# Sums of g's blocks for the seven-product matrix multiply: from VectorE to accumulating transfers on GpSimd's queue, with signs chosen anew

## The chip, the cores and the metric

The kernel runs on one core of one Trainium2 chip. The metric is device microseconds of one execution. A core has five engines that run in parallel, each taking its own instructions in program order: TensorE (PE in the profile; its weight loads are PEld), VectorE (DVE), ScalarE (ACT), GpSimd (POOL) and SyncE (SP). Transfers are issued from an engine's queue and carried out by 16 DMA engines. Engines wait for each other, and for transfers, by semaphores.

## The reference

Two blocks follow one another. The first is a linear attention (RWKV6): per head and time step, `y[t] = r[t] @ (state + (u*k[t]) outer v[t])` and `state = w[t] * state + k[t] outer v[t]`, with 4 batches, 8 heads, 768 steps and 48 channels. Its output, taken as `x` of 3072 tokens by 384, goes through a two-layer network:

```python
h = x @ w_in                                   # w_in: 384 x 2048
g = 0.5 * h * (1.0 + erf(h * inv_sqrt2))       # exact GELU
out = (g @ w_out).astype(np.float32)           # w_out: 2048 x 384
```

Everything is float32. The change lies in how `g @ w_out` is computed.

## The kernel before

**Chunks.** The 3072 tokens are worked in eight chunks of T = 384 tokens, numbered 0 to 7. `attention(x + 1)` is generated in step with `mlp(x)`: both are Python generators, and a string of letters per chunk (`PLAN`) says which one issues its next piece. A letter "." takes a step of `mlp`, "f" and "s" take steps of the attention, "l" a load, "w" and "x" sums of the weights and of x. So the order of every engine's instructions is written out by hand; no scheduler moves them. Chunk 7's `mlp` has no attention left beside it and ends the kernel.

**g.** In `mlp(x)` the activations lie transposed: 2048 rows of g as 16 blocks of 128 partitions, by tokens. Four tiles `gs[0]` to `gs[3]` hold four such blocks each (`[128, 4, 384]`). In even chunks the last 128 tokens are kept in a tile `alone` instead, which waits there for the odd chunk behind it. So an odd chunk has 128 + 128 tokens and then a second pair: its own last 128 and the 128 of `alone`.

**Seven products.** For a pair of 128-token blocks, `g @ w_out` is a 2 x 2 by 2 x 2 block product, done in seven products instead of eight (Winograd's form of Strassen's scheme). With a00, a01 for the first token block (its two halves of the 2048) and a10, a11 for the second, the sums on g's side are

    s1 = a10 + a11,   s2 = s1 - a00,   s3 = a00 - a10,   and later  s2 <- a01 - s2

and on the side of the weights three sums `t` in `sums`, made once (`w_sums`, L873, and `first_sum`, L882). One product is eight matmuls of 128x192, one for each block row of 128 (`product`, L1235, its matmul is L1237); the profile shows two records for a float32 matmul, so a product is "x16". The order within a pair, all on the in-order TensorE, is: p1 (a00), o2 (a11), o1 (a01), **fourth: s2**, fifth: s1, sixth: s3, **seventh: the later s2**. In an odd chunk the second pair follows with five more: a11, s2, s1, s3, later s2. Each sum has two halves, k = 0 and 1, one tile of 128 x 512 float32 (256 KB) each; a product reads half 0 in its first four matmuls and half 1 in its last four.

**Where the sums are made.** `of_g(k)` (L997) makes s1, s2 and s3 of half k with three VectorE instructions (L1003, L1005, L1007). In chunks 2 to 6 half 0 is called for after the last but one group of h, and half 1 right after p1, since the last GELUs (`rest`, called between the halves of p1) come only then. In chunk 1 both are called in the h loop (L1231). In chunk 7 `of_g(0)` is the entry "sums" of `ORDER15` and `of_g(1)` follows the last own product. The later s2 is L1291, after the fifth product has been issued. An odd chunk's second pair gets its sums at L1302 and L1303 (after the sixth product), L1311 (after the seventh) and L1350. s1 lies in the tiles named f, s2 in those named e, s3 in the one named s; tile names in the profile are of the buffer's first user.

Of the kernel before, what the change touches and what calls it, by code (L numbers as in the profile page):

```python
# [17 lines left out]
AF = mybir.ActivationFunctionType  # L18
ALU = mybir.AluOpType
# [45 lines left out]
def kernel(  # L65
# [25 lines left out]
    nc = tc.nc  # L91
# [41 lines left out]
    def bank(name="o_ps"):  # L133
        return ps.tile([128, BANK], F32, name=name, tag="mm", bufs=2)
# [13 lines left out]
    alone = bufs[0][:, ALL:ALL + NF * 128].rearrange("p (f t) -> p f t", f=NF)  # L148
# [132 lines left out]
    for i, h in enumerate(QUARTERS[:1]):  # L281
        for a in range(3):
            w_q = (3 - a) * C // 4
            z = q_ints[1 if a == 0 else 2]
            o = i * C if a < 2 else i * C + C // 2
# [580 lines left out]
    HF, HM = NF // 2, DM // 2  # L866
    FG = 4
    sums, s3_sb = [], []

    def w_quarter(b, c, k):  # L870
        return w_out_sb[:, b * HF + k * FG:b * HF + (k + 1) * FG, c * HM:(c + 1) * HM]

    def w_sums():  # L873

        sums.extend(cv.tile([128, HF, HM], F32, name="t", tag="raw", bufs=AHEAD) for _ in range(3))
        for out_, x, y in ((0, (0, 1), (0, 0)), (1, (1, 1), (0, 1)), (0, (1, 1), 0), (2, (1, 0), 0)):
            for k in range(2):
                o = sums[out_][:, k * FG:(k + 1) * FG]
                nc.vector.tensor_sub(o, w_quarter(*x, k), sums[y][:, k * FG:(k + 1) * FG] if isinstance(y, int) else w_quarter(*y, k))
                yield  # L880

    def first_sum():  # L882
        for k in range(2):
            nc.vector.tensor_sub(w_quarter(0, 1, k), w_quarter(0, 1, k), w_quarter(0, 0, k))
            yield


# [2 lines left out]
    s_of, x_sums, s12_of, s_both = [], [], {}, []  # L890
# [91 lines left out]
    def mlp(x):  # L982
# [5 lines left out]
        waits, ends = x % 2 == 0, x % 2 == 1  # L988
        gs = {}
# [4 lines left out]
        def store(row0, o_sb, c0=0):  # L994
            nc.sync.dma_start(out=out[row0:row0 + 128, c0:c0 + o_sb.shape[1]], in_=o_sb)

        def of_g(k):  # L997

            s1.append(s12_of["s1"][k])
            s2.append(s12_of["s2"][k])  # L1000
            s3.append(s3_sb[0][:, k * FG:(k + 1) * FG])
            a00, a10, a11 = (gs[g][:, :, a:a + 128] for g, a in ((k, 0), (k, 128), (k + 2, 128)))
            nc.vector.tensor_add(s1[k], a10, a11)  # L1003
            yield
            nc.vector.tensor_sub(s2[k], s1[k], a00)  # L1005
            yield
            nc.vector.tensor_sub(s3[k], a00, a10)  # L1007
            yield

        def multiply(o, lhsT, rhs, start=False):  # L1010
# [4 lines left out]
        def h_halves():  # L1015
# [101 lines left out]
            for _ in of_g(0):  # L1117
                pass
# [93 lines left out]
        s1, s2, s3 = [], [], []  # L1212
# [22 lines left out]
        def product(o, lhs, rhs, start=False):  # L1235
            for j in range(HF):
                nc.tensor.matmul(o, lhsT=lhs(j), rhs=rhs(j), start=start and j == 0, stop=(j == HF - 1),  # L1237
                                 skip_group_check=True)
                if j == HF // 2 - 1:
                    yield  # L1240

        def of_sums(s):
            return lambda j: s[j // FG][:, j % FG, :]

        def of_t(i):
            return lambda j: sums[i - 1][:, j, :]

        def of_blocks(a, b):
            return lambda j: block(a, b, j)
# [4 lines left out]
        def of_w(b, c):  # L1254
            return lambda j: w_out_sb[:, b * HF + j, c * HM:(c + 1) * HM]

        def psum():
            return bank()[:, 0:HM]

        def two_rows():  # L1260
            return [wk.tile([128, DM], F32, name="o_sb", bufs=2) for _ in range(2)]
# [3 lines left out]
        if halves:  # L1265
            o_sb = two_rows()
            p1, u2, u3 = (wk.tile([128, HM], F32, name=name, bufs=1) for name in ("p1", "u2", "u3"))
            o1, o2 = psum(), psum()
            for _ in product(o1, of_blocks(0, 0), of_w(0, 0), True):
                yield  # L1270
                for z in late:
                    z()
            nc.scalar.copy(out=p1, in_=o1)
            if late:
                for _ in of_g(1):
                    pass
            yield
            yield from product(o2, of_blocks(1, 1), of_t(3), True)
            nc.scalar.copy(out=o_sb[1][:, 0:HM], in_=o2)
            yield  # L1280
            yield from product(o1, of_blocks(0, 1), of_w(1, 0))
            nc.scalar.copy(out=o_sb[0][:, 0:HM], in_=o1)
            yield
            yield from product(o2, of_sums(s2), of_t(1), True)
            nc.vector.tensor_add(u2, o2, p1)
            yield
            yield from product(o1, of_sums(s1), of_w(0, 1), True)
            nc.scalar.copy(out=o_sb[1][:, HM:], in_=o1)
            for k in range(2):

                nc.vector.tensor_sub(s2[k], gs[k + 2][:, :, 0:128], s2[k])  # L1291
            yield
            yield from product(o2, of_sums(s3), of_t(2))
            nc.vector.tensor_add(u3, o2, p1)
            for c in range(2):
                z = o_sb[1][:, c * HM:(c + 1) * HM]
                nc.vector.tensor_add(z, z, u3)
            store(row0 + 128, o_sb[1])
            if ends:
                s1 = s12_of["s1"]  # L1300
                for k in range(2):
                    nc.vector.tensor_add(s1[k], gs[k][:, :, 256:], gs[k + 2][:, :, 256:])  # L1302
                    nc.vector.tensor_sub(s3[k], alone[:, k * FG:(k + 1) * FG], gs[k][:, :, 256:])  # L1303
            yield
            yield from product(o1, of_sums(s2), of_w(1, 1))
            nc.vector.tensor_add(o_sb[0][:, HM:], o1, u2)
            store(row0, o_sb[0])
            if ends:
                s2 = s12_of["s2"]
                for k in range(2):  # L1310
                    nc.vector.tensor_sub(s2[k], s1[k], alone[:, k * FG:(k + 1) * FG])  # L1311
            yield
        else:
            o_ps = [bank()[:, 0:DM] for _ in range(2)]
            for f in range(NF):
                for i, o in enumerate(o_ps):
                    nc.tensor.matmul(o, lhsT=block(i, f // HF, f % HF), rhs=w_out_sb[:, f, :],
                                     start=(f == 0), stop=(f == NF - 1))
                if f < NF - 1:
                    yield  # L1320
            for i, o in enumerate(o_ps):
                o_sb = wk.tile([128, DM], F32, name="o_sb", bufs=2)
                nc.scalar.copy(out=o_sb, in_=o)
                store(row0 + i * 128, o_sb)
            yield

        if waits:
            _, o2, o1 = psum(), psum(), psum()
            o_sb = wk.tile([128, DM], F32, name="o_sb", bufs=2)
            yield from product(o2, of_alone(0), of_w(0, 0), True)  # L1330
            nc.scalar.copy(out=p1_alone, in_=o2)
            yield
            yield from product(o1, of_alone(1), of_w(1, 0), True)
            nc.vector.tensor_add(o_sb[:, 0:HM], o1, p1_alone)  # L1334
            store(row0 + 256, o_sb[:, 0:HM])
            yield
        elif ends:
            o_sb = two_rows()
            p1, u2, u3 = p1_alone, *(wk.tile([128, HM], F32, name=name, bufs=1) for name in ("u2", "u3"))
            o2, o1 = psum(), psum()  # L1340
            yield from product(o1, of_blocks(2, 1), of_t(3), True)
            nc.scalar.copy(out=o_sb[1][:, 0:HM], in_=o1)
            yield
            yield from product(o2, of_sums(s2), of_t(1), True)
            nc.vector.tensor_add(u2, o2, p1)
            yield
            yield from product(o1, of_sums(s1), of_w(0, 1), True)
            nc.scalar.copy(out=o_sb[1][:, HM:], in_=o1)
            for k in range(2):
                nc.vector.tensor_sub(s2[k], alone[:, HF + k * FG:HF + (k + 1) * FG], s2[k])  # L1350
            yield
            yield from product(o2, of_sums(s3), of_t(2))
            nc.vector.tensor_add(u3, o2, p1)
            for c in range(2):
                z = o_sb[1][:, c * HM:(c + 1) * HM]
                nc.vector.tensor_add(z, z, u3)  # L1356
            store(row0 + 256, o_sb[1])
            yield
            yield from product(o1, of_sums(s2), of_w(1, 1))
            nc.vector.tensor_add(o_sb[0][:, 0:HM], o1, u2)  # L1360
            store(row0 - T + 256, o_sb[0][:, 0:HM], HM)
            yield
# [114 lines left out]
```

## Time and profile before

| | |
|---|---|
| runs | 589.09, 589.76, 591.12 us; median 589.76 |
| profiled execution | 591.24 us, span of the instructions 589.5 us |
| granted TensorE clock, mean | 0.997 |
| busy: PE / PEld / DVE / ACT / POOL | 571.5 / 508.5 / 462.6 / 275.7 / 8.0 us |
| transfers | 46.80 MB, mean 79 GB/s |
| VectorE's sums of g | L1003 9.6, L1005 9.7, L1007 9.6 (x14 each), L1291 9.0 (x14), L1302 5.5, L1303 5.5, L1311 5.1, L1350 5.1 (x8 each) us |

Busy time is the time in which an engine had an instruction in work. A line "A <- B" of the waits says for what the engine A stood idle, in total, how often, and the longest once. The chain of work that ended last is followed back from the last instruction. Times in timelines are microseconds from the span's start.

### The profile page before, as it was taken

To read this page: it belongs to the slowest core of one execution; us is meant where nothing else is said; L and a number is where in the kernel's file an instruction comes from. 1 tells how busy PE (TensorE), PEld (TensorE's weight loads), DVE (VectorE), ACT (ScalarE), POOL (GpSimd) and SP (SyncE) were. 2 spreads that over 40 slices of the span, in tenths; PEclk is the share of its full clock that TensorE was granted. 3 is DMA by queue.
4 is the path that set the end of the run, shared out by engine and by line. 5 is a ranking of instruction groups with operands and counts; after the bars stand their busy time and mean duration, and the time that the engine had idled before them with its cause. 6 is when DMAs were issued, how large, how long until landed. Compare 5 with 4: busy or idle time off the path is not lost. (4 is left out here: it accounts for less than half of the span.)

```text
span 589.5 us, 17409 instructions
## 1 busy us (share of the span) xinstructions
PE 571.5 (97%) x7497; PEld 508.5 (86%) x7509; DVE 462.6 (78%) x907; ACT 275.7 (47%) x640; POOL 8.0 (1%) x21
## 2 busy tenths in 40 slices
PE   5789999999999999999999999999999999999998
PEld 3566666766799999999999999999999999999997
DVE  5879767988969987787859987688768998985532
ACT  2267889323612458045461468235461465523400
POOL 3100000000000000000000000000000000000000
PEclk9999999999999999999999999999999999999999
DMA  6649571020152201341023410421015200210000
GB/s 238 193 156 342 193 267 56 31 91 1 23 147 78 77 34 28 101 126 38 0 40 104 126 37 16 100 79 43 2 26 170 73 2 2 41 39 8 1 14 34
DMA packets 51004, 46.80 MB, mean 79 GB/s; under 512 B 31728, under 2 KB 36080, under 8 KB 50928
## 3 DMA queue, kind: packets, MB, share of 16 engines
q1 hardware_dynamic: 50832, 45.62, 25.5%
q8 instruction: 59, 0.97, 0.7%
q14 instruction: 17, 0.14, 0.1%
q10 hardware_dynamic: 96, 0.07, 0.1%
HBM read 36.24 MB, written 4.72 MB: 69 GB/s over the span
## 5 line engine op out<-in xcount | busy, mean ns | idle before, releaser
L1011 PE MATMUL h_ps<-xT,w_in_sb 128*128 128x192 f32 x408 | 81.2, 330 | 0.5 <-DVE o_sb L1334 0.3
L1011 PEld LDWEIGHTS h_ps<-xT,w_in_sb 128*128 128x128 f32 x408 | 67.8, 190 | 3.5 <-ACT g L1043 1.2
L1223 PE MATMUL h_ps<-xT,w_in_sb 128*128 128x384 f32 x192 | 64.4, 490 | 0.4 <-DMA xT<-ysb 0.4
L1223 PEld LDWEIGHTS h_ps<-xT,w_in_sb 128*128 128x128 f32 x192 | 35.8, 190 | 24.6 <-DMA xT<-ysb 1.0
L1237 PE MATMUL o_ps<-w_out_sb,g 128*128 128x192 f32 x224 | 39.5, 326 | 0.0
L1237 PEld LDWEIGHTS o_ps<-w_out_sb,g 128*128 128x128 f32 x224 | 37.0, 190 | 0.3
L620 ACT COPY a_sb<-d 32x256 f32<-32x256 f32 (+8 forms) x90 | 32.6, 362 | 4.6 <-PE d L604 3.1
L465 PEld LDWEIGHTS d<-rkw 64*64 64x64 f32 x1152 | 20.8, 147 | 16.0 <-issue 11.2
L1237 PE MATMUL o_ps<-w_out_sb,f 128*128 128x192 f32 x176 | 31.7, 330 | 0.0
L465 PE MATMUL d<-rkw 64*64 64x64 f32 (+1 forms) x1152 | 23.5, 234 | 8.2 <-DMA rkw<-in_rkw_dram 3.9
L1237 PE MATMUL o_ps<-t,g 128*128 128x192 f32 x176 | 31.4, 329 | 0.0
L1237 PE MATMUL o_ps<-w_out_sb,e 128*128 128x192 f32 x176 | 31.3, 328 | 0.0
L1237 PE MATMUL o_ps<-t,s 128*128 128x192 f32 x176 | 30.9, 327 | 0.0
L1237 PE MATMUL o_ps<-t,e 128*128 128x192 f32 x176 | 30.9, 327 | 0.0
L637 DVE COPY_PREDICATED a_sb<-quarter,d 128x480 f32<-128x480 uint8 (+5 forms) x54 | 23.2, 439 | 8.6 <-PE d L604 7.3
L764 DVE SCALAR_TENSOR_TENSOR st<-st,tot_sb,kv_ps 128x48 f32<-128x48 f32 x160 | 28.9, 259 | 0.9 <-PE kv_ps L749 0.8
L1011 PE MATMUL u_ps<-s,w_in_sb 128*128 128x192 f32 x160 | 29.5, 327 | 0.0
L1237 PEld LDWEIGHTS o_ps<-t,g 128*128 128x128 f32 x176 | 28.7, 190 | 0.4
L1237 PEld LDWEIGHTS o_ps<-w_out_sb,f 128*128 128x128 f32 x176 | 28.7, 190 | 0.4
L1237 PEld LDWEIGHTS o_ps<-w_out_sb,e 128*128 128x128 f32 x176 | 28.8, 190 | 0.3
L1237 PEld LDWEIGHTS o_ps<-t,s 128*128 128x128 f32 x176 | 28.8, 190 | 0.1
L1237 PEld LDWEIGHTS o_ps<-t,e 128*128 128x128 f32 x176 | 28.8, 190 | 0.1
(236 smaller groups left out, 1166.8 us busy)
## 6 DMA issues: line engine op xcount, KB each, us to landing
rkw<-in_rkw_dram SPq DMA_DIRECT2D x54, 256.0 KB, 3.9
raw<-in_w_out_dram SPq DMA_DIRECT2D x8, 768.0 KB, 4.8
v_in<-in_v_dram SPq DMA_DIRECT2D x8, 584.0 KB, 4.7
raw<-in_w_in_dram SPq DMA_DIRECT2D x5, 768.0 KB, 6.9
out_dram<-o_sb SPq DMA_DIRECT2D x20, 192.0 KB, 2.5
rkw<-kx SPq DMA_DIRECT2D x72, 48.0 KB, 2.0
rkw<-in_rkw_dram SPq DMA_DIRECT2D x6, 384.0 KB, 6.6
raw<-in_w_in_dram SPq DMA_DIRECT2D x9, 256.0 KB, 4.6
```

The lines of the kernel that those rows point to most:

```text
L465: nc.tensor.matmul(d[half[p], g, n * width:(n + 1) * width], lhsT=kc[half[g], b, i, p], rhs=right(half[g], b, i, p), start=True, stop=True)
L620: nc.scalar.copy(out=at[z, g, first:behind, (a + 1) * h:], in_=d[z, :, :, to] if g == slice(None) else d[z, :, to])
L637: nc.vector.copy_predicated(out=an[:, :, :, :, (a + 1) * h:], mask=mask.to_broadcast(data.shape), data=data)
L764: nc.vector.scalar_tensor_tensor(out=stq[:, q, c], in0=stq[:, q, c - 1] if c else b4[:, q, NC - 1], scalar=totq[:, q, c:c + 1], in1=kvs[q ...
L1011: nc.tensor.matmul(o, lhsT=lhsT, rhs=rhs, start=start, stop=True, skip_group_check=True)
L1223: nc.tensor.matmul(h_ps, lhsT=w_in_sb[:, f // FI, j, f % FI * 128:(f % FI + 1) * 128], rhs=xT[:, j, :], start=(j == 0), stop=(j == NJ - 1))
L1237: nc.tensor.matmul(o, lhsT=lhs(j), rhs=rhs(j), start=start and j == 0, stop=(j == HF - 1), skip_group_check=True)
```

## The change

The signs of the seven-product scheme are chosen so that every sum on g's side is a plain sum: s1 = a10 + a11, s2 = s1 + a00, s3 = a10 + a00, later s2 <- s2 + a01. The weights' sums (`w_sums`, `first_sum`) take the other signs with as many instructions as before, the copy of the fifth product out of PSUM is negated (an `activation` of ScalarE with scale -1 in place of a `copy`), and o_sb - u3 takes the place of o_sb + u3.

A plain sum can be made by a transfer that adds into its destination. These are issued from GpSimd's queue (`accumulate`). In `of_g`, ScalarE copies a00 to s2 and, for half 0, a10 to s1; then transfers add a11 to s1 (half 0 only; half 1's s1 stays on VectorE), s1 to s2, and a00 to a10, where s3 now lies in place, inside g. The later s2 is a transfer. For an odd chunk's second pair ScalarE copies a10 to s1, now in the tile that held s3, and two transfers for each half make s1 and s3; these are issued right after the fourth product and before the later s2's transfers; s2 stays on VectorE, its later form is a transfer.

```diff
+        def accumulate(o, z):
+            nc.gpsimd.dma_start(out=o, in_=z, accum_op=ALU.add)
+
+        def three_sums(k, a00, a10, a11, s1, s2):
+            nc.scalar.copy(out=s2, in_=a00)
+            if k == 0:
+                nc.scalar.copy(out=s1, in_=a10)
+                yield
+                accumulate(s1, a11)
+            else:
+                yield
+                nc.vector.tensor_add(s1, a10, a11)
+            yield
+            accumulate(s2, s1)
+            accumulate(a10, a00)
+            yield
 ...
-            nc.vector.tensor_add(s1[k], a10, a11)
-            nc.vector.tensor_sub(s2[k], s1[k], a00)
-            nc.vector.tensor_sub(s3[k], a00, a10)
+            s3.append(a10)
+            yield from three_sums(k, a00, a10, a11, s1[k], s2[k])
 ...  in the products, behind the fourth:
+            if ends:
+                s1_ends, s3_ends = [s3_sb[0][:, k * FG:(k + 1) * FG] for k in range(2)], []
+                for k in range(2):
+                    a00, a10, a11 = alone[:, k * FG:(k + 1) * FG], gs[k][:, :, 256:], gs[k + 2][:, :, 256:]
+                    s3_ends.append(a10)
+                    nc.scalar.copy(out=s1_ends[k], in_=a10)
+                    accumulate(s1_ends[k], a11)
+                    accumulate(a10, a00)
 ...  behind the fifth:
-            nc.scalar.copy(out=o_sb[1][:, HM:], in_=o1)
+            nc.scalar.activation(out=o_sb[1][:, HM:], in_=o1, func=AF.Copy, scale=-1.0)
             for k in range(2):
-                nc.vector.tensor_sub(s2[k], gs[k + 2][:, :, 0:128], s2[k])
+                accumulate(s2[k], gs[k + 2][:, :, 0:128])
 ...  behind the sixth:
-                nc.vector.tensor_add(z, z, u3)
+                nc.vector.tensor_sub(z, z, u3)
-            if ends:
-                s1 = s12_of["s1"]
-                for k in range(2):
-                    nc.vector.tensor_add(s1[k], gs[k][:, :, 256:], gs[k + 2][:, :, 256:])
-                    nc.vector.tensor_sub(s3[k], alone[:, k * FG:(k + 1) * FG], gs[k][:, :, 256:])
 ...  behind the seventh, for the second pair:
-                    nc.vector.tensor_sub(s2[k], s1[k], alone[:, k * FG:(k + 1) * FG])
+                    nc.vector.tensor_add(s2[k], s1[k], alone[:, k * FG:(k + 1) * FG])
 ...  in the second pair:
-                nc.vector.tensor_sub(s2[k], alone[:, HF + k * FG:HF + (k + 1) * FG], s2[k])
+                accumulate(s2[k], alone[:, HF + k * FG:HF + (k + 1) * FG])
```

## The prediction, as it was made before the result was known

> **What bounds the kernel.** I read the page's busy shares and its chain, then the waits of TensorE, then timelines.
>
> ```profile
> PE 571.5 (97%) x7497; PEld 508.5 (86%) x7509; DVE 462.6 (78%) x907; ACT 275.7 (47%) x640; POOL 8.0 (1%) x21
> ```
>
> TensorE is busy 97% of the span. The waits of TensorE alone tell what the other 3% are:
>
> ```profile
> PE d L465 <- DMA rkw<-in_rkw_dram: 3.9, 1, 3.9
> ...
> PE y_ps L790 <- DVE st L764: 0.7, 2, 0.4
> ...
> PE h_ps L1011 <- DVE o_sb L1334: 0.3, 1, 0.3
> PE h_ps L1011 <- DVE o_sb L1360: 0.2, 1, 0.2
> ```
>
> The long ones lie in the start. Behind 60 us TensorE's in-order stream almost never stops, so VectorE, though 78% busy, bounds nothing but those last rows. Taking work off VectorE can win little; whatever makes TensorE wait is paid in full. The order of TensorE's instructions stays the same: the question is whether each new sum is ready when its product comes.
>
> **What goes.** VectorE loses 5 of 6 instructions of `of_g` in 7 chunks (35), L1302 and L1303 (16), L1291 (14) and L1350 (8): 73 of about 0.69 us, 50 us. What does TensorE get of that? By VectorE's timeline, the 0.37 us wait for st at 316.5 comes behind a packed run that begins with four L1302 and L1303 at 308.95, and the 0.22 us wait for L1360 at 465.5 behind one with L1350 at 459.2. From start to start of TensorE's instructions these two pauses are 0.54 and 0.38 us longer than the usual pitch, and one of 0.20 follows the first. **I count -1.1 us.** The pauses at 380.9 (VectorE had itself just waited for kv) and 394.1 (it had waited for a transfer of xT) stay; if they went too, it would be -2.0; if the next row behind VectorE were late instead, 0.
>
> **What comes on ScalarE:** 29 copies of 128x512. The nearest row from SBUF to SBUF is L573, 128x384 in 510 ns; by width I take 0.62 us (between 0.51 and 0.68). In chunk 2 two of them land in a full queue:
>
> ```profile
> 229.56 0.48 ACT L1047 COPY o_sb<-h_ps 128x384 f32<-128x384 f32 x1
> 229.94 1.63 ACT L620 COPY a_sb<-d 32x128 f32<-32x128 f32 x6
> 231.57 0.49 ACT L1043 ACTIVATE g<-u_ps 128x384 f32<-128x384 f32 x1
> 231.96 0.30 ACT L1040 ACTIVATE g<-g 128x128 f32<-128x128 f32 x1
> 232.16 0.41 ACT L1043 ACTIVATE rkw<-g 128x256 f32<-128x256 f32 x1
> 232.47 0.30 ACT L1040 ACTIVATE g<-g 128x128 f32<-128x128 f32 x1
> ```
>
> They go between L1047 and L620, so all that is below them comes 1.24 us later. The last GELU ends near 234.0; the product that reads its blocks 6 and 7 is there at 231.57 + 6 x 0.325 = 233.5. That is a wait of 0.45 us, in chunk 4 again; in chunks 3, 5 and 6 ScalarE idles 2.1 us before L1043, which hides them. I don't add it: the waits below are longer and lie behind it in the same stream. The negated copy costs what the plain one did (L1181, an `activate` of 128x384 with a scale, 0.47; a copy of that shape 0.48).
>
> **What comes on GpSimd's queue:** 73 accumulating transfers of 256 KB. Two figures are needed and the trace has neither: L, from issue to landing, and q, GpSimd's time to issue one. Nearest rows:
>
> ```profile
> rkw<-in_rkw_dram SPq DMA_DIRECT2D x54, 256.0 KB, 3.9
> out_dram<-o_sb SPq DMA_DIRECT2D x20, 192.0 KB, 2.5
> rkw<-kx SPq DMA_DIRECT2D x72, 48.0 KB, 2.0
> rkw<-in_rkw_dram SPq DMA_DIRECT2D x6, 384.0 KB, 6.6
> ```
>
> The columns are size and median us to landing. 48 KB from SBUF to SBUF need 2.0, so L isn't below that; a store of 192 KB needs 2.5. An accumulate reads its destination as well and moves runs of 512 B; 384 KB in six transfers in a row took 6.6, my upper end. I take the row of the same size, **L = 3.9**. SP's timeline has twelve `rkw<-kx` issues in 8.00 us, so **q = 0.67** (ends 0.1, hidden by L, and 2, which I add to the slow case).
>
> The Trainium skill (DMA: Bandwidth & Descriptors, "Anatomy of one DMA") fits transfers issued from GpSimd by 2.0 us plus bytes over 436e3 per us; an estimate from it is 2.6 for 256 KB, and by that the sum would be the quick case below. The same page ("Latency and other measured facts") gives GpSimd's path about 1 us to the first byte where SP's has 0.6; that speaks against the change, and L would be an estimated 4.3, the sum near +11. No transfer of this trace shows either.
>
> **The critical pair.** In `of_g` half 0 needs two transfers in series: a11 into s1 (issued when both ScalarE copies are done, at time c), and, only after that has landed, s1 into s2. TensorE's fourth product needs s2 at time f. Half 0 waits if c + 2L > f. Half 1's transfer into s2 stands in the queue behind half 0's two, so it lands at c + 2L + 2q, and is needed at f + 1.30 (half a product). From the timelines, with L = 3.9, q = 0.67:
>
> - chunk 1: c = 157.0 + 1.24 = 158.3, f = 165.33: half 0 late by 0.8 (half 1 is needed only at 168.4, behind the kv matmuls).
> - chunk 2: c = 229.94 + 1.24 = 231.2, f = 236.77: late by 2.2, half 1 by 2.3. I count 2.3.
> - chunk 4: the same stretch at 365.3 and 372.14: 2.3.
> - chunks 3 and 5: c = 290.5 and 426.6, f = 299.95 and 436.07, since attention work lies between: both fit.
> - chunk 6: c = 500.7, f = 507.84: half 1 late by 0.7.
> - chunk 7: the GELU of p10B ends at 555.52, c = 556.76, f = 562.96, nothing beside it: half 1 late by 1.7.
>
> ```profile
> 231.57 2.76 PE L1237 MATMUL o_ps<-t,g 128*128 128x192 f32 x16
> 234.17 2.76 PE L1237 MATMUL o_ps<-w_out_sb,g 128*128 128x192 f32 x16
> 236.77 2.76 PE L1237 MATMUL o_ps<-t,e 128*128 128x192 f32 x16
> ```
>
> This is chunk 2: second, third and fourth product back to back, 2.60 us each; `t,e` is the fourth. Sum: 0.8 + 2.3 + 2.3 + 0.7 + 1.7 = **7.8 us**.
>
> **The later s2.** Its old half 0 is free in the middle of the fourth product and it is needed three half products and a product later, 6.5 us at least: L alone fits. But in odd chunks four transfers of the second pair are issued first. Chunk 3: ScalarE's first copy ends at 301.1, four issues take 2.7, landing 303.8 + 3.9 = 307.7, needed at 307.75; chunk 5: 439.9 + 3.9 = 443.8 against 443.87. Cost nothing, but with no slack left: each further us of L or of four q is paid there. In the second pair 6.5 us hide L. s3 and the second pair's s1 have a product more than that. s3 now lies in g, so g's tiles stay in use until the sixth product; the next chunk's first write comes more than 2.6 us later. Weight sums: as many instructions as before.
>
> **Sum.** 7.8 - 1.1 = +6.7. On the profiled execution: span 589.5 to 596.2, its own time 591.24 to 597.9. That execution is 1.48 above the median of the runs; on the median, 589.76 + 6.7 = **596.5 us**.
>
> **Rivals.**
> - *Quick transfers: not slower.* Place: chunks 2 and 4, the shortest cover. With L below (236.77 - 231.2) / 2 = 2.8 nobody waits and VectorE's pauses go: 588.7, down to 587.8 with all of them, up to 589.6 if the two GELU delays are paid. For it: 192 KB in 2.5 and 48 KB in 2.0. Against: the double reading, the short runs, and `rkw<-kx` moves that hold the DMA engines at 0.33 to 0.44 of their time just in 230 to 238 (windows of 2 us).
> - *Slow transfers: much slower.* L = 5.5 (halfway from 3.9 to 6.6, about): 4.0 + 2 x 5.5 + 3.9 + 4.8 at the fourth products of chunks 1, 2, 4, 6 and 7, 1.6 and 1.5 in 3 and 5 (there the later s2 is late too): 26.7 - 1.1, 615. At 6.6 it is 631. With q = 2, four issues ahead of the later s2 alone cost some 5 us in each of chunks 3 and 5. For it: loads share the engines (at 448 to 450 us they are full), and GpSimd has never issued a transfer in this trace. Against: the short stores.
> - *The change does little of what it says*: it would need VectorE to keep its 73 instructions; the order of the changed instructions shows them gone, so I give it nothing.
>
> **Chances.** Forecast with L from 3.3 to 4.7 (591.3 to 605.8): 0.41; quick 0.33; slow 0.26. About 0.3%, 1.8 us, can be told from no change. Quick is faster by more only if most pauses go: 0.13 of its 0.33; the rest, and 0.02 of the forecast's edge, is no change (0.22); slower 0.65. The range takes quick from 588 and slow up to 618, which leaves out some 0.06 below and 0.12 above.
>
> **What would show it.** Right: a new row TensorE `o_ps` waiting for a transfer into e or f, about 2 us, once in chunks 2 and 4, less in 1, 6 and 7, none in 3 and 5; VectorE near 412 us busy, ScalarE near 294; landings on GpSimd's queue near 3.9. Wrong if L is below 2.8 or above 5, if the waits sit at the seventh product (then q is the price), or if TensorE waits for ScalarE's GELUs.

## The result and the profile after

The changed kernel takes **658.71 us** (median of 4 runs, 655.96 to 662.54) where the kernel before takes 589.42: a ratio of 1.1171, interval 1.1134 to 1.1209. Forecast was 596.5, with a range to 618. The profiled execution took 660.42 us, its span is 658.6, 69.1 more than before. The changed kernel's lines stand 14 lower: L1237, the product's matmul, is L1251; `accumulate` is L1007.

The page, busy shares and the granted clock in 40 slices:

```profile
PE 595.3 (90%) x7497; PEld 526.2 (80%) x7509; DVE 420.0 (64%) x834; ACT 291.1 (44%) x669; POOL 94.2 (14%) x94
...
PEclk9899999999879996999979999999989999899879
```

VectorE is busy for 420.0 us where about 412 were forecast, ScalarE for 291.1 (294). TensorE executes the same 7497 matmuls but is busy for 23.8 us more, and its granted clock, 0.997 on average before, is 0.956: a slice that shows 6 to 8 holds stretches at half clock. The other 45 us are idle. The waits of TensorE (total, times, longest):

```profile
PE o_ps L1251 <- DMA e<-g: 22.9, 4, 6.8
PE o_ps L1251 <- DMA e<-f: 20.1, 11, 3.8
PE d L465 <- DMA rkw<-in_rkw_dram: 3.3, 1, 3.3
...
PE o_ps L1251 <- ACT rkw L733: 2.5, 1, 2.5
```

The first row is the seventh product waiting for the later s2, the second the fourth product waiting for s2. The last row is the fourth product of chunk 6: it starts at 560.78, a copy of ScalarE and the transfer into e both end within the 0.13 us before, so I count it with the second row, 22.6 together. Of these waits only the fourth product's were forecast, at 7.8. The short waits behind VectorE (L1011 for `o_sb`, 0.5 in all) are gone, and the two for `st` are one of 0.3.

The transfers, packets and bytes of a queue with the share of 16 engines' span, and issues with their median time to landing:

```profile
q0 software_dynamic: 30096, 19.14, 23.5%
...
e<-f POOLq DMA_DIRECT2D x14, 256.0 KB, 5.0
g<-g POOLq DMA_DIRECT2D x14, 256.0 KB, 7.2
e<-g POOLq DMA_DIRECT2D x14, 256.0 KB, 11.0
rkw<-kx SPq DMA_DIRECT2D x72, 48.0 KB, 3.8
```

All 256 KB, yet 5, 7 and 11 us: what a transfer takes depends on what it is issued behind. The queue's share gives the price: 23.5% of 658.6 us is 155 us of all 16 engines, and by 73 transfers (19.14 MB) **2.1 us each**. The attention's moves on SP's queue went from 2.0 to 3.8.

Where in the kernel? From the first product of a chunk to that of the next (chunk 7: to the end), chunks 1 to 7:

```
before    70.1   60.9   74.5   61.6   74.1   56.4   34.3
after     83.2   71.1   85.4   68.0   83.5   62.1   47.6
more      13.1   10.2   10.9    6.4    9.4    5.6   13.3     sum 68.9
```

All of it lies here, 9.4 to 13.3 in odd chunks and 5.6 to 10.2 in even ones. Chunk 7 shows how, having nothing beside it. GpSimd's timeline (start, us up to the end of issuing, [idle before]):

```profile
612.85 1.30 POOL L1007 DMA_DIRECT2D f<-g  x1 [44.60 <-ACT g L1205]
617.62 0.89 POOL L1007 DMA_DIRECT2D e<-f  x1 [3.47 <-DMA f<-g]
...
621.73 4.26 POOL L1007 DMA_DIRECT2D s<-g  x1
...
623.74 6.17 POOL L1007 DMA_DIRECT2D e<-g  x2
```

and TensorE's, fourth (two halves), fifth, sixth and seventh product:

```profile
621.29 2.15 PE L1251 MATMUL o_ps<-t,e 128*128 128x192 f32 x8 [2.29 <-DMA e<-f]
624.86 2.93 PE L1251 MATMUL o_ps<-t,e 128*128 128x192 f32 x8 [1.42 <-DMA e<-f]
627.58 3.42 PE L1251 MATMUL o_ps<-w_out_sb,f 128*128 128x192 f32 x16
630.83 2.76 PE L1251 MATMUL o_ps<-t,g 128*128 128x192 f32 x16
637.16 5.46 PE L1251 MATMUL o_ps<-w_out_sb,e 128*128 128x192 f32 x16 [3.56 <-DMA e<-g]
```

The trace's landing of each transfer of the chunk stands beside its issue here:

```
issued  612.85 617.62 618.17 618.93 619.48 620.23 620.98 621.73 622.48 623.74 628.09
landed  617.08 621.15 623.23 624.82 627.16 629.32 631.55 633.65 635.18 637.02 638.48
        f      e      g      e      g      s      g      s      g      e      e
```

From 617.62 to 622.48 they are issued every 0.55 to 0.75 us, the last two later, as the fourth product sets the old halves free; they land every 1.5 to 2.3. The later s2 (the last two) is issued with six transfers in front of it that have not landed, needs 13.3 us for its half 0 where 3.9 was forecast. The seventh product would follow the sixth at 633.43 (630.83 + 2.60) and starts at 637.16, 3.73 us late. It then takes 5.25 us where it took 2.60 before. One-microsecond windows (busy shares of PE, PEld, DVE, ACT, POOL; then the granted clock, DMA share, GB/s):

```profile
634.00:635.00 1.00, 0.00 (x0) 0.00 (x0) 0.63 (x2) 0.00 (x0) 0.00 (x0) 1.00 1.33 150
...
636.00:637.00 1.00, 0.00 (x0) 0.00 (x0) 0.00 (x0) 0.00 (x0) 0.00 (x0) 0.50 1.09 195
...
638.00:639.00 1.00, 1.00 (x5) 1.00 (x4) 0.00 (x0) 0.00 (x0) 0.00 (x0) 0.50 0.17 53
...
643.00:644.00 1.00, 1.00 (x8) 1.00 (x7) 1.00 (x3) 0.00 (x0) 0.00 (x0) 1.00 0.08 28
```

The DMA engines' time is full (a share above 1; the packets' times overlap) until 637, shortly before the last landing at 638.48. The clock is halved 2.1 us into the wait (635:636 has 0.86 on average) and stays so for 5 us of work behind it: five records a microsecond in place of eight.

### The profile page after: what moved, and what is told of

Same layout as the page of the kernel before. It is cut to its first block, busy times and chain, and to the rows that moved or that the text cites. A ratio compares the mean times of both kernels' runs of the same rounds, so it can differ in the third digit from the quotient of the medians.

```text
span 658.6 us, 17575 instructions
## 1 busy us (share of the span) xinstructions
PE 595.3 (90%) x7497; PEld 526.2 (80%) x7509; DVE 420.0 (64%) x834; ACT 291.1 (44%) x669; POOL 94.2 (14%) x94
## 3 DMA queue, kind: packets, MB, share of 16 engines
q0 software_dynamic: 30096, 19.14, 23.5%
## 5 line engine op out<-in xcount | busy, mean ns | idle before, releaser
L1007 POOL DMA_DIRECT2D f<-g x7 | 9.2, 1316 | 420.6 <-ACT f L1013 285.9
L1237 PE MATMUL h_ps<-xT,w_in_sb 128*128 128x384 f32 x192 | 64.4, 490 | 0.4 <-DMA xT<-ysb 0.3
L1251 PE MATMUL o_ps<-t,g 128*128 128x192 f32 x352 | 63.0, 329 | 0.4 <-ACT g L1054 0.4
L1251 PE MATMUL o_ps<-t,e 128*128 128x192 f32 x176 | 41.7, 394 | 22.6 <-DMA e<-f 20.1
L1251 PE MATMUL o_ps<-w_out_sb,e 128*128 128x192 f32 x176 | 40.5, 393 | 22.9 <-DMA e<-g 22.9
L1251 PEld LDWEIGHTS o_ps<-t,g 128*128 128x128 f32 x352 | 57.7, 190 | 1.5 <-ACT g L1054 1.0
L1251 PEld LDWEIGHTS o_ps<-t,e 128*128 128x128 f32 x176 | 35.7, 230 | 26.7 <-DMA e<-f 10.8
L1251 PEld LDWEIGHTS o_ps<-w_out_sb,e 128*128 128x128 f32 x176 | 36.9, 235 | 24.4 <-issue 24.0
L1237 PEld LDWEIGHTS h_ps<-xT,w_in_sb 128*128 128x128 f32 x192 | 35.8, 190 | 24.6 <-DMA xT<-ysb 0.9
L1251 PE MATMUL o_ps<-w_out_sb,g 128*128 128x192 f32 x224 | 39.5, 326 | 0.0
L1299 DVE TENSOR_TENSOR u<-o_ps,p 128x192 f32<-128x192 f32 x7 | 2.5, 358 | 55.2 <-PE o_ps L1251 50.5
L1251 PEld LDWEIGHTS o_ps<-w_out_sb,g 128*128 128x128 f32 x224 | 37.0, 190 | 0.3
L764 DVE SCALAR_TENSOR_TENSOR st<-st,tot_sb,kv_ps 128x48 f32<-128x48 f32 x160 | 29.1, 257 | 5.2 <-PE kv_ps L749 5.1
L465 PE MATMUL d<-rkw 64*64 64x64 f32 (+1 forms) x1152 | 23.8, 235 | 8.1 <-DMA rkw<-in_rkw_dram 3.3
L1007 POOL DMA_DIRECT2D e<-g x14 | 28.2, 2442 | 15.6 <-PE o_ps L1251 9.7
L1310 ACT ACTIVATE o_sb<-o_ps 128x192 f32<-128x192 f32 x7 | 2.3, 331 | 60.1 <-PE o_ps L1251 60.1
```

The costliest lines, as they stand in the source:

```text
L465: nc.tensor.matmul(d[half[p], g, n * width:(n + 1) * width], lhsT=kc[half[g], b, i, p], rhs=right(half[g], b, i, p), start=True, stop=True)
L764: nc.vector.scalar_tensor_tensor(out=stq[:, q, c], in0=stq[:, q, c - 1] if c else b4[:, q, NC - 1], scalar=totq[:, q, c:c + 1], in1=kvs[q ...
L1007: nc.gpsimd.dma_start(out=o, in_=z, accum_op=ALU.add)
L1237: nc.tensor.matmul(h_ps, lhsT=w_in_sb[:, f // FI, j, f % FI * 128:(f % FI + 1) * 128], rhs=xT[:, j, :], start=(j == 0), stop=(j == NJ - 1))
L1310: nc.scalar.activation(out=o_sb[1][:, HM:], in_=o1, func=AF.Copy, scale=-1.0)
```

## The experiments

The theories that the expectations name. **A**: a transfer takes about 2 us of the 16 DMA engines, one is served behind the other, and TensorE waits for the last of a pile. **B**: each accumulating transfer takes some 11 us by itself. **C**: the loss comes from the rest of the change (ScalarE's copies, the negated copy, s3 inside g, the signs). **D**: GpSimd's issuing, 0.75 us each, is the price. **E**: waiting itself makes TensorE slow afterwards. The kernel before took 589.1 to 590.1 beside these runs. A time without a number of runs is that of one execution.

**1. All 73 sums on VectorE again**, with the new signs, copies and places.

```diff
-            nc.gpsimd.dma_start(out=o, in_=z, accum_op=ALU.add)
+            nc.vector.tensor_add(o, o, z)
```

> The changed kernel with each accumulating transfer replaced by a VectorE addition into the same place; the signs, ScalarE's copies and the order of all queues stay. If the transfers are the whole loss (theory A: they are served one behind the other by the DMA engines, some 2 us each, and TensorE waits for the last of a pile), the time falls from 658.7 to that of before within 2 us: 588 to 592, with TensorE's waits for transfers gone and its granted clock back at 0.997. The rival that ScalarE's 29 copies, the negated copy or s3 lying inside g delay the stream (theory C) leaves it above 600.

Measured: 592.19 (median of 10), ratio 1.0032, interval 1.0007 to 1.0056, clock 0.997. No product waits for a transfer any more. C falls as the main cause: everything but the transfers costs about 2 us, the transfers some 66.5.

**2. The second pair's 16 on VectorE**, the other 57 as they were.

```diff
-                    accumulate(s1_ends[k], a11)
-                    accumulate(a10, a00)
+                    nc.vector.tensor_add(s1_ends[k], s1_ends[k], a11)
+                    nc.vector.tensor_add(a10, a10, a00)
```

> Only the 16 transfers of the second pair's s1 and s3 (odd chunks, issued ahead of the later s2) become VectorE additions; the other 57 stay. TensorE doesn't wait for those 16 themselves. Theory A (a pile served in order): the later s2's two transfers then have five ahead of them instead of nine, land some 8 us earlier, and the waits ahead of the seventh product in chunks 1, 3, 5 and 7 (6.1, 7.0, 6.8 and 3.7 us, and a slow TensorE for some 5 us behind each) go: 658.7 to about 622 to 634. Theory B (each transfer takes its 11 us by itself, whatever else is on the queue): the seventh product waits as before, above 650. Theory D (GpSimd's issuing at 0.75 us each is the price): 16 x 0.75 = 12 us less at most, about 647.

Measured: 634.64. The later s2's transfers are still there, but no seventh product waits for them; the fourth ones do, in this row of its waits:

```profile
PE o_ps L1251 <- DMA e<-f: 21.2, 10, 3.8
```

With four transfers fewer ahead of it the later s2 is in time. That speaks for A against B, by which it would be as late. D isn't excluded by this alone: the time is just outside A's span, though 12 us below D's 647.

**3. All 73 kept, the later s2's issued ahead of the second pair's.**

```diff
+            yield
+            yield from product(o1, of_sums(s1), of_w(0, 1), True)
+            nc.scalar.activation(out=o_sb[1][:, HM:], in_=o1, func=AF.Copy, scale=-1.0)
+            for k in range(2):
+                accumulate(s2[k], gs[k + 2][:, :, 0:128])
             if ends:
...  (the same five lines go behind this block)
```

> All 73 transfers stay; in odd chunks the two of the later s2 are put ahead of the four of the second pair (and ScalarE's copies for these behind the negated copy). Theory A: the later s2 lands with four transfers fewer ahead of it, some 8 us earlier, so that the seventh products hardly wait, but the second pair's sums come later: they are needed 8 us after the seventh, so most of it is hidden, 630 to 640. Theory B: no change, above 650. Theory D: the issuing is as much as before, but 4 x 0.75 = 3 us earlier for the later s2, four times: about 646.

Measured: 651.67, not the 630 to 640 of A, and above the 650 that B named. But B's mechanism isn't what happened: as A says, the seventh product waits for no transfer any more, and chunks 7 and 1 fall by 4.3 and 8.5 us; chunks 3 and 5 stay (86.1 and 83.2). Its waits show what took the place:

```profile
PE o_ps L1251 <- DMA e<-f: 22.9, 12, 3.8
PE kv_ps L749 <- DMA out_dram<-o_sb: 8.0, 1, 8.0
PE kv_ps L749 <- DMA rkw<-kx: 4.2, 2, 3.1
...
PE o_ps L1251 <- DVE e L1327: 2.3, 1, 2.3
```

The pile is as large as before, and in chunks 3 and 5 the attention's transfers of SP's queue stand in it. The 8.0 us, in chunk 3, are put down to a store, but they end at 334.87, 0.14 us behind the landing of an `rkw<-kx` move that took 8.1 us, so I take that for their cause. My sizes for A left these moves out.

**4. Transfers by themselves.** This kernel computes nothing of the reference and writes zeros. Bursts; the first three begin when the one before has landed, some of the later ones while the one before is still landing, so their figures are the times between landings in a row:

```python
for n in (1, 2, 8):
    burst(n, add, goal, runs)     # 512-byte runs at the source: z[:, :, 128:256] of [128, 4, 384]
for n in (1, 8):
    burst(n, add, goal, flat)     # contiguous
for n in (1, 8):
    burst(n, add, places, runs)   # runs on both sides
burst(8, copy(nc.gpsimd), goal, runs)
...
```

> The transfers by themselves, with nothing else running: the kernel only writes zeros to its output and issues bursts of 1, 2 and 8 transfers of 256 KB between SBUF tiles, each burst behind the landing of the one before: accumulating with runs of 512 B at the source, with contiguous 2 KB rows, with runs of 512 B on both sides; then eight plain copies from GpSimd's queue and eight from SP's, with runs and without. Theory A: one alone lands in 3.5 to 5 us, and in a burst of eight the landings follow each other by about 2 us (the last at about 18); an accumulate costs about twice a plain copy. Theory B: in a burst of eight all land 7 to 11 us behind their own issue and a single one does too. Theory D: landings follow each other by the 0.55 to 0.75 us of the issue, the last at about 9 us.

Measured: one alone lands after 4.4 us, of two the second after 5.4, of eight the last after 13.8, each counted from its own issue. The eight with runs:

```
issued   31.38 32.13 32.88 33.63 34.38 35.13 35.88 36.63
landed   35.87 38.05 40.33 42.61 44.97 46.90 48.75 50.42
```

Eight of each kind, mean time between landings (accumulating with runs on both sides: 2.03):

```
                            runs of 512 B    contiguous
accumulating, GpSimd             2.08           1.45
plain copy, GpSimd               1.14           0.76
plain copy, SP                   0.99           0.65
```

With TensorE and ScalarE idle and VectorE nearly so, the burst has the spacing of the kernel: A holds and B falls. Issuing takes 0.75 us each (0.54 contiguous), faster than they land. GpSimd's instructions overlap and take longer than that; a row of its timeline has the eight, and one of the windows (VectorE, GpSimd, clock, DMA share, GB/s) what follows:

```profile
31.38 10.40 POOL L109 DMA_DIRECT2D goal<-wide  x8 [4.35 <-DVE wide L117]
...
44.00:46.00 2.00, 0.16 (x1) 0.00 (x0) 1.00 1.29 140
```

That is 1.30 us each, still less than 2.08, and when GpSimd has done its part the DMA engines are still full, for GpSimd's eighth ends at 41.78 and the eighth lands at 50.42. So D falls. Accumulating costs about twice a plain copy.

**5. `of_g`'s 35 on VectorE**, 38 transfers left.

```diff
-                accumulate(s1, a11)
+                nc.vector.tensor_add(s1, s1, a11)
...
-            accumulate(s2, s1)
-            accumulate(a10, a00)
+            nc.vector.tensor_add(s2, s2, s1)
+            nc.vector.tensor_add(a10, a10, a00)
```

> The other half undone: the five transfers of of_g (35 in all) become VectorE additions, ScalarE's copies stay; the second pair's four and the later s2's two stay transfers. Theory A with the burst's figures (4.4 us for one, 2.1 us more for each behind it): the fourth products no longer wait; even chunks are as before; in odd chunks six transfers in a row from some 1 us behind the fourth product's start land the later s2 near 4.4 + 4 x 2.1 = 13 us later, needed at 7.8 us: a wait of some 5 us and a slow TensorE behind it in chunks 1, 3, 5 and 7: 590 + 4 x 7.5 = 620, between 612 and 628. If the second pair's transfers only hurt because of the five ahead of them: below 600.

Measured: 626.76, as A expects. Even chunks are back at 63.0, 62.3 and 56.4; odd ones wait at the seventh product:

```profile
PE o_ps L1251 <- DMA e<-g: 24.6, 4, 7.5
```

**6. Only the later s2 by transfers** (22), no copies by ScalarE: the kernel before with the new signs.

```diff
-                nc.vector.tensor_sub(s2[k], gs[k + 2][:, :, 0:128], s2[k])
+                accumulate(s2[k], gs[k + 2][:, :, 0:128])
...  (likewise in the second pair; signs as in the change)
```

> The kernel before with the new signs and only the later s2 (22 additions) by transfers; all else on VectorE as before, without ScalarE's 29 copies. Theory A: two transfers with an empty queue land 4.4 and 6.5 us behind the first issue, or 4.4 behind each issue when they are issued 1.3 us or more apart, and each has 6.5 us before its product: next to no waits, 588 to 591, at best 1 below before, by the pauses that VectorE's lighter load takes away. If any transfer of GpSimd's queue costs the kernel (port, queue, the attention's transfers): above 595.

Measured: 594.03 (11 runs), ratio 1.0080, interval 1.0055 to 1.0105: slower, and I had expected no difference. No product waits for a transfer. But two rows of its waits have grown:

```profile
PE kv_ps L749 <- DMA rkw<-kx: 2.8, 3, 2.0
...
PE y_ps L832 <- DVE fence L802: 2.0, 4, 0.9
```

The 48 KB moves from SP, 2.0 us to landing, take up to 5.7 in chunks 3 and 5 when one of the 22 is beside them. So a transfer with ample time of its own still delays its neighbours. How much of the 4.7 us that is stays open: the signs may be a part (run 1's 2 us), and run 1 has the first wait as well, without a single transfer from GpSimd, when its last move lands after 3.8 us beside SP's own load and store:

```profile
PE kv_ps L749 <- DMA rkw<-kx: 1.3, 1, 1.3
```

**7. The 73 adds on GpSimd itself**, no transfers.

```diff
-            nc.gpsimd.dma_start(out=o, in_=z, accum_op=ALU.add)
+            nc.gpsimd.tensor_tensor(out=o, in0=o, in1=z, op=ALU.add)
```

> The changed kernel with the 73 additions computed by GpSimd itself in place of transfers. The trace has a GpSimd memset of 128x512 in 0.53 us; an addition reads twice and takes at least that. The chain of half 0 becomes two additions in series instead of two transfers of 4 us: if one takes below 2.5 us, no product waits and the time is 590 to 596; at 4 us or more it is about that of the transfers where these were alone. Theory A says the loss is in the transfer engines: far below 658.7 in any case. If GpSimd's instructions as such hold up VectorE, VectorE's busy time rises above 440 us and the time above 600.

Measured: 599.44. An add takes 1.30 to 1.56 us, so the pile doesn't form; yet the time is above the 590 to 596 that I expected. VectorE, with 73 instructions fewer, is busy for 444.4 us where the changed kernel has 420.0; run 11 shows a likely reason.

**8 and 9. TensorE kept busy in the waits**, in chunk 7 alone, by matmuls whose result nobody reads. First too few, then enough:

```diff
+            if x == NX - 1:
+                u = bank_u(0)
+                for _ in range(16):
+                    nc.tensor.matmul(u, lhsT=zeros[:, 0:128], rhs=zeros, start=True, stop=True)
             yield from product(o1, of_sums(s2), of_w(1, 1))
...  first run: 10 ahead of the fourth product, 16 ahead of the seventh
...  second run: 12 ahead of the fourth, 11 between its halves, 34 ahead of the seventh
```

> The changed kernel; in chunk 7 alone TensorE works off 10 idle matmuls (zeros, into a free bank, read by nobody) ahead of the fourth product and 16 ahead of the seventh, in stretches in which it waited for 2.5 and 3.7 us. In the changed kernel the matmuls behind these waits came at a pitch of 320 ns instead of 162 for some 5 us. Theory E, that the waiting itself makes TensorE slow afterwards: with work in the wait the pitch stays 162 or 163, and chunk 7, from p1's first matmul to the end, shrinks from 47.5 us to 42 to 44. If the slow pitch comes from the transfers running beside it: it stays at 320, and chunk 7 at 47 or more.

Measured: 657.95, chunk 7 48.2, which is the rival's number; but the filler is too short, so it is inconclusive:

```profile
635.61 4.55 PE L1251 MATMUL o_ps<-w_out_sb,e 128*128 128x192 f32 x16 [1.93 <-DMA e<-g]
```

TensorE is still idle for 1.93 us ahead of the seventh product. That starts at full clock, and the matmuls are at 320 ns only from 636.4 to 639.9.

> As the changed kernel with all 73 transfers, but in chunk 7 alone TensorE is given matmuls whose result nobody reads: 12 ahead of the fourth product, 11 between its halves, 34 ahead of the seventh, at 216 ns each by the run before; these are long enough for the whole of the waits. Theory E (waiting itself makes TensorE slow afterwards): the transfers land when they did, the seventh product starts where it did, but the matmuls of the fourth, fifth and seventh products then keep the pitch of 162 ns in place of 320, a product takes 2.6 us in place of 4 to 5, and chunk 7 takes 42 to 44.5 us in place of 47.6; the time is 654 to 656. Rival (the traffic of the transfers slows TensorE, or its clock drops by some other rule): the pitch is 320 in the same places though TensorE was never idle, and chunk 7 stays at 47 to 48.

Measured: 653.98, chunk 7 46.7, above the 42 to 44.5 expected. No matmul of the seven products in chunk 7 is at 320 ns; the third line is the seventh product, which takes 2.60 us to the next one in place of 5.25:

```profile
623.41 2.76 PE L1251 MATMUL o_ps<-t,g 128*128 128x192 f32 x16
626.01 7.50 PE L1333 MATMUL u_ps<-zeros 128*128 128x512 bf16 x33
633.35 2.76 PE L1251 MATMUL o_ps<-w_out_sb,e 128*128 128x192 f32 x16
```

And the windows show the clock at 1.00 both in the stretch of the filler, with the DMA engines as full as after, and behind it:

```profile
630.00:631.00 1.00, 1.00 (x7) 0.41 (x5) 0.00 (x0) 0.00 (x0) 0.00 (x0) 1.00 1.28 184
...
634.00:635.00 1.00, 1.00 (x8) 1.00 (x8) 0.00 (x0) 0.00 (x0) 0.00 (x0) 1.00 0.00 0
```

The mechanism of E is shown: the waiting halves the clock, not the traffic. The size was missed. The later s2's first half landed 26.04 us after the chunk's start, in the changed kernel 25.99; but my filler ran 1.86 us past it, and what it saved at the fourth and fifth products was lost in the wait for the seventh anyway. The sum comes out: 47.6 less 2.65 at the seventh product, with 1.86 for the filler, is 46.8. Chunk 2, not edited, took 3.2 us less in this run, so the whole time is no evidence.

**10. Runs, bytes and neighbours.** Again no kernel of the reference; it writes zeros. Eight accumulating transfers of each form, then moves of 48 KB from SP beside eight of them, and alone:

```python
burst(8, add, goal, [z[:, :, 128:256] for z in wide])                          # 512 runs of 512 B
burst(8, add, [z[:, 0:2] for z in goal], [z[:, 0:2, 128:256] for z in wide])   # 128 KB
...                                                                            # 1024 of 256 B, 256 of 1 KB
for o, z in zip(goal, wide):
    add(o, z[:, :, 128:256])
moves(12)
```

> No kernel of the reference: it only writes zeros and measures transfers. Bursts of eight accumulating transfers from GpSimd: 256 KB in 512 runs of 512 B (again), 128 KB in 256 runs of 512 B, 256 KB in 1024 runs of 256 B, 256 KB in 256 runs of 1 KB; then twelve moves of 48 KB from SP alone, and the same twelve beside eight accumulating transfers. Theory A (served one behind the other by the DMA engines): from the first burst's 2.08 us for 512 runs and 1.45 for 128 rows, 0.63 us for 384 more runs; so 1.04 between landings for 128 KB, 2.9 for 256-B runs, 1.66 for 1-KB runs, if runs are the price; if only the bytes count, 2.08 for all three of 256 KB; if a transfer has a fixed price, 128 KB takes more than 1.5. The moves of 48 KB: median some 2 to 4 us from issue to landing alone, 6 us and more beside the eight (they share the engines), if the traffic of the transfers is what held the attention's moves; unchanged if those were late for another reason.

Measured, time between landings: 2.03 (512 B), 1.22 (128 KB), 2.79 (256 B), 1.66 (1 KB). The number of runs is a price: from 128 to 1024 runs 256 KB go from 1.45 to 2.79, some 1.5 ns a run. So are the bytes: 256 runs cost 1.22 with 128 KB and 1.66 with 256 KB; GpSimd's own instructions take 9.73 us for the eight of 128 KB, 1.22 each, so they may pace that burst, and the engines could need less. The moves of SP's queue land after 1.9 alone and after 2.6 to 8.6 beside the eight: the neighbours' delay of runs 3 and 6, without the rest of the kernel.

**11. The kernel before with L1302 and L1303 on GpSimd's own adds**: the term of -1.1 us by itself.

```diff
-                    nc.vector.tensor_add(s1[k], gs[k][:, :, 256:], gs[k + 2][:, :, 256:])
-                    nc.vector.tensor_sub(s3[k], alone[:, k * FG:(k + 1) * FG], gs[k][:, :, 256:])
+                    nc.gpsimd.tensor_tensor(out=s1[k], in0=gs[k][:, :, 256:], in1=gs[k + 2][:, :, 256:], op=ALU.add)
+                    nc.gpsimd.tensor_tensor(out=s3[k], in0=alone[:, k * FG:(k + 1) * FG], in1=gs[k][:, :, 256:], op=ALU.subtract)
```

> The kernel before, with its own signs and no transfer added, but the 16 sums of the second pair (L1302 and L1303 in its numbering) made by GpSimd's own adds, 1.3 to 1.6 us each by an earlier run, in place of VectorE's. This is the term of -1.1 us of the prediction by itself: if taking these sums off VectorE removes the pauses counted there (0.54 and 0.20 us behind L1302 and L1303; the 0.38 us behind L1350 stays), the wait for st of 0.37 us is gone from TensorE's waits and the time falls by 0.4 to 0.8 us, to about 588.5 of 589.2. Rival: the next row behind VectorE is late instead, or GpSimd's adds slow VectorE's beside them: no gain, 589 to 590.5, and the wait for st stays or another of its size appears. A ratio below 0.997 or above 1.003 would fall outside both.

Measured: 591.04 (11 runs), ratio 1.0024, interval 1.0002 to 1.0046: no gain. VectorE lost 16 instructions of 0.69 us, 11 us, and is still busy for 461.5 us (462.6 before). VectorE's timeline, in the kernel before

```profile
174.21 3.04 DVE L404 SCALAR_TENSOR_TENSOR kx<-rkw,u_sb 128x384 f32<-128x384 f32 x4
```

and here, while GpSimd adds from 169.1 to 176.5:

```profile
171.91 6.01 DVE L404 SCALAR_TENSOR_TENSOR kx<-rkw,u_sb 128x384 f32<-128x384 f32 x4
```

An instruction of 0.89 us takes up to 1.91 beside GpSimd's add, and L1297's of 0.36 up to 1.43; the nine that were slowed take 8.2 us longer than they do by themselves. L764's, of which one input lies in PSUM, keep their 0.26 beside it. The Trainium skill (SBUF — State Buffer, "SBUF: two separate sides") gives VectorE and GpSimd one shared pair of ports, held for a whole instruction, and among VectorE's instructions that need it has those with two inputs in SBUF; by that rule such an instruction would wait for GpSimd's to end, and the trace agrees. One wait of TensorE for st (0.3) is left of two (0.7), but a wait of 1.2 us for VectorE's u L1294 has come. So the rivals hold: another row is late instead, and GpSimd's adds slow VectorE's.

No version beats the kernel before. The nearest are this one and run 1.

## Why the prediction was wrong, point by point

**The step that failed** is the one under *The later s2*: "Cost nothing, but with no slack left", and in it "four issues take 2.7, landing 303.8 + 3.9". It takes a transfer's time to be a latency L that overlaps with the others', so that only GpSimd's issuing q stands between two. The trace of before had the warning: the six loads of 384 KB took 6.6 us each in the median (not the six together), those of 256 KB 3.9, and twelve `rkw<-kx` moves held the DMA engines at 0.33 to 0.44; I used both only for L. The missing term is the **service time**, 2.08 us an accumulating transfer (run 4). With it, four transfers ahead cost 8.3 us of engines' time, not 2.7 of issuing, and the later s2 is late by 6.1, 7.0, 6.8 and 3.7 us in chunks 1, 3, 5, 7. The line "each further us of L or of four q is paid there" named the place; "if the waits sit at the seventh product (then q is the price)" named a wrong price, as issuing was measured at 0.55 to 0.75.

**The critical pair** was found in the right place, at the fourth products, but sized too small, for the same reason: 7.8 us forecast (by the prediction's own rows chunk 7's term is 1.6, not 1.7), 22.6 in the rows of the waits. Chunk 7, from c (612.85, first issue): half 0 was forecast at c + 2L = 7.8 us and landed at 8.3. Half 1 was forecast at c + 2L + 2q = 9.1 and landed at 12.0, since half 0's s3 (`g<-g`) is served in between. In chunk 2 half 0 is late by 4.0 us, and half 1 once more:

```profile
254.55 2.90 PE L1251 MATMUL o_ps<-t,e 128*128 128x192 f32 x8 [3.83 <-DMA e<-f]
258.74 2.93 PE L1251 MATMUL o_ps<-t,e 128*128 128x192 f32 x8 [1.30 <-DMA e<-f]
```

From the first product to the fourth chunk 2 takes 4.45 us more than before (the 4.0 and 0.45 for GELUs), from the fourth to the fifth 5.28 more, with half 1's wait and the half clock in it, and in the seventh 0.51 more: together the 10.2 lost, where 2.3 were forecast.

**L**: 3.9 was fair for a transfer that stands alone (`f<-g` 4.2 to 5.0, run 4 4.4). The estimate of 2.6 from the Trainium skill's fit (DMA: Bandwidth & Descriptors, "Anatomy of one DMA") is too low here. The other estimate, 4.3, by the first-byte figure of the same page ("Latency and other measured facts"), agrees with these rows, though no run here shows a first byte. With 4.4 in place of 3.9 the prediction's own sum gives an estimated 602: L wasn't the main error.

**The clock** was not thought of. 91 of the records of the seven products' matmuls have a pitch near 320 ns in place of 162.5 in the changed kernel, none in the kernel before: 14.3 us of 69, though some of it lies inside waits that follow, and what share is paid isn't settled. In chunk 7 the fourth product's wait was 2.3 us long, and the half clock came some 3.1 us after its start, when TensorE was at work again; ahead of the seventh product it came 2.1 us into the wait. Behind the kernel's first 60 us every wait of TensorE of 2.3 us or more has half clock in it or right behind it; the longest that has none is 1.7 us (chunk 3's fourth product). In run 8 one of 1.93 us was enough and another, of 2.01, was not. The Trainium skill (TensorE: Matmul & The Clock Gate, "Part 1: The HAM clock gate") has TensorE fall to half rate after an idle window of about 3.4 us and return after as long a window of work; the half rate and the slow 5 us fit that, but shorter waits were enough here.

**The neighbours**: "loads share the engines" stood in the slow rival as an argument for it and was not priced. `rkw<-kx` landed after up to 9.0 us instead of 2.0.

**VectorE's pauses** (-1.1): their waits did shrink after, from 1.2 to 0.3, but nothing of that could be measured in the time; run 11, which tried part of it alone, gained nothing. **ScalarE's copies**: 0.62 us as forecast. The GELU delay is there as forecast: in chunks 2 and 4 the second product takes 0.45 us more from start to start (two waits of 0.2 in the rows). Copies, signs and the negated copy together cost about 2 us (run 1), where the forecast had nothing; which of them isn't settled.

**The slow rival** (615, up to 631 at L = 6.6) had the right sign, but its cause, a larger L, isn't what the runs show: one transfer alone lands after 4.4 us, not 5.5 or 6.6. In the range's upper end the pile was missing.

## What to carry to other kernels

A transfer has two prices, its latency and the time that the DMA engines need to serve it; where more are issued within one latency, the second adds up, and whoever is last in the pile, or in another queue beside it, pays. Before work is moved to transfers, multiply their number in the tightest stretch by the service time of one (read it from landings in a row, with its runs and whether it accumulates) and compare with the time until the first reader. Where TensorE will wait for some 2 us or more again and again (2.3 here), add the slow matmuls behind each wait.

## What the runs showed of the hardware that I had not expected

- An accumulating transfer of 256 KB within SBUF from GpSimd, with runs of 512 B, takes 4.4 us alone and 2.08 in a row (1.45 contiguous); a plain one from the same queue 1.14 and 0.76, from SP 0.99 and 0.65.
- Within SBUF, too, short runs cost: some 1.5 ns for each run of an accumulating transfer, and SP's copies go from 0.65 to 0.99 with runs of 512 B.
- SP's 48 KB moves go from 1.9 us to as much as 8.6 beside eight accumulating transfers of GpSimd's queue.
- TensorE at half clock after a wait of 2.3 us (1.93 in run 8), from 622.07 to 628.9, 6.8 us, in chunk 7.
- VectorE's instruction of 0.89 us took up to 1.91 beside an add on GpSimd, so that 11 us taken off VectorE lowered its busy time by 1.1 only.
